# A six-layer cross network on one core: tiles of two groups woven at the start, output tails by one DMA turn and a Pool copy, fillers on TensorE, products moved in the last job

## The chip, the cores and the metric

The kernel runs on one core of a Trainium2 chip. The metric is device time in microseconds (us), less is better. A profile's span, from first to last instruction, is about 2 us shorter than the time of the same execution. The engines are called as in the profile: PE is TensorE (PEld its weight loads), ACT is ScalarE, DVE is VectorE, POOL is GpSimd, SP is SyncE, which here only issues DMAs.

## The reference, cut to what matters

```python
B, Din, L = 16384, 416, 6            # bf16 throughout
def reference(x0, ws, bs):           # x0 [B, Din], ws [L, Din, Din], bs [L, Din]
    x = x0
    for l in range(L):
        proj = jnp.einsum('bd,de->be', x, ws[l]) + bs[l]
        x = x0 * proj + x
    return x
```

## The kernel before: the parts that matter here

The batch is cut into 8 groups of 2048 rows. A *job* (g, l) is layer l of group g; the jobs are interleaved so that a group's next layer mostly finds its input done. The 416 features are three tiles of 128 and a *tail* of 32. A tile of a job, written (g, l)i, takes 12 full products of 128x512 on PE and 4 *row products* for the 32 tail inputs. Two neighbouring tiles share one stretch of row products. The tails of several jobs are computed together. ACT adds the bias while it empties PSUM; DVE multiplies by x0 and adds x.

```python
def load_group(g):                         # input, turned by DMA; SP issues in order
    for t in range(NT):
        add("sp", ... dma_start_transpose(x0s[s] tile t, x0[rows, t*P:(t+1)*P]))
    add("sp", ... dma_start_transpose(Tb[:, :], x0[rows, D - P:D]))
    for j in range(NJ):                    # four copies: the tail's quarters into place
        add("sp", ... dma_start(x0s[s][q, XW:XW + CH], Tb[P - T32:P, ...]))
...
load_nat(...)                              # group 0 comes in as rows and is turned on PE
load_w3(0, "sp"); load_wm(1, "sp"); load_w3(1, "sp"); load_group(1)
...
keep_busy(14, 7)                           # 14 products of no use, before the first input
def first_job(): ...                       # (0,0): turns, 3 tiles, then its tails
...
for jb in order[1:-1]:                     # order: (0,0), (0,1), (1,0), (0,2), (1,1), ...
    for i in range(NT): items.append(("tile", jb, i)) ...

def output(g):                             # groups 0 to 6: turn back by DMA, then store
    if g < LAST - 1: turn(0); turn(1)
    for j in range(NJ):                    # the tails: four turns of 32x512
        add("sp", ... dma_start_transpose(ost[:, j*KK:(j+1)*KK, NT*P:D], x3s[s3][q, :]))
    if g == LAST - 1: turn(0); turn(1)
    turn(2)
    add("sp", ... dma_start(out rows of g, ost))        # 1.66 MB
...
# the last job (7,5) is computed in row order, so that it can be stored without turns:
turn_main(0, bka, (0, 1)); turn_tails(0, bka)   # turns of x by PE
nat_rows(0, bkb, True)                          # row products and bias
turn_main(0, bka, (2,))                         # needs x tile 2, which is the last one made
rows_out(0, bka)                                # ACT and DVE copy the turned x out
layer_full(0, bkb)                              # 12 products, ACT copies, DVE multiplies and adds
turn_main(1, ...) ... layer_full(1) ... layer_full(2) ... layer_full(3), with stores between
```

A source line number differs between kernels when lines were added above it; the lines shown below name what they write and read.

## Time and profile before

| | before |
|---|---|
| time, median | 492.34 us at first (491.89 to 492.51), later runs 491.56 to 493.71 |
| PE busy, share of the span | 474.3 us, 97% |
| DVE, ACT, POOL busy | 405.8, 343.4, 11.9 us |
| steady state, two tiles | 5.29 us of full products and 0.54 us of row products |

The profile's page gives the span, the busy time of each engine and the shares of the chain of waits that ended last:

```profile
span 490.6 us, 8035 instructions
PE 474.3 (97%) x3191; PEld 203.2 (41%) x3245; DVE 405.8 (83%) x713; ACT 343.4 (70%) x372; POOL 11.9 (2%) x37
PE 90%; DVE 4%; ACT 2%; issue 2%; DMA 1%; SPq 0%; DVEq 0%
```

PE is the limit nearly everywhere, and a change that removes no products can only win where PE stands still or runs slowly. Those places are the two ends. The timeline has start, duration, engine, instruction and count, and in brackets the idle time before and what ended it. The start:

```profile
4.84 0.82 PE L516 MATMUL ps<-ident,x 128*128 128x128 bf16 x6 [0.60 <-DMA x<-in_x_dram]
8.53 1.49 PE L516 MATMUL ps<-ident,x 128*128 128x128 bf16 x12
10.28 0.84 PE L516 MATMUL ps<-ident,x 128*128 128x128 bf16 x12
...
20.79 0.83 PE L443 MATMUL ps<-x,wm 128*32 128x512 bf16 x12
25.77 0.61 PE L430 MATMUL ps<-x,w 32*128 32x512 bf16 x8 [0.41 <-DVE x L408]
26.32 5.35 PE L418 MATMUL ps<-x,wm 128*128 128x512 bf16 x23
43.04 0.40 PE L430 MATMUL ps<-x,w 32*128 32x512 bf16 x4 [0.35 <-DVE x L408]
```

The same twelve transposes take 1.49 us at 8.53 us and 0.84 us at 10.28 us: PE's clock rises between them. The first job's tail products start at 20.79 us. PE waits twice for an x-tail from DVE, before 25.77 us and before 43.04 us. The end:

```profile
463.50 5.00 SPq L604 DMA_TRANSPOSE ost<-x  x4
466.76 1.35 DVE L386 TENSOR_TENSOR tw<-tw,x 128x1024 bf16<-128x1024 bf16 x2
468.54 7.92 SPq L595 DMA_TRANSPOSE ost<-x  x3
470.73 0.86 ACT L753 ACTIVATE x<-ps 128x832 bf16<-128x832 bf16 x1 [1.02 <-PE ps L731]
472.93 2.10 ACT L789 ACTIVATE x<-ps 128x416 bf16<-128x416 f32 x4
476.02 1.62 ACT L753 ACTIVATE x<-ps 128x832 bf16<-128x832 bf16 x2 [0.99 <-PE ps L740]
478.72 0.37 SPq L617 DMA_DIRECT2D out_dram<-ost  x1
485.89 0.38 ACTq L803 DMA_DIRECT2D out_dram<-x  x1
```

SP issues seven output turns of group 6 in one row, from 463.50 to 476.46 us, and its store at 478.72 us, when the last job's own stores are about to begin. The last store is issued at 485.89 us, and the span still runs until 490.6 us. The DMA view of the last 15 us shows why (size, then us from issue to landing):

```profile
out_dram<-ost SPq DMA_DIRECT2D x1, 1664.0 KB, 6.7
out_dram<-x SPq DMA_DIRECT2D x1, 832.0 KB, 7.0
out_dram<-x SPq DMA_DIRECT2D x1, 104.0 KB, 4.5
out_dram<-x ACTq DMA_DIRECT2D x1, 104.0 KB, 3.8
```

A store of 104 KB needs 3.8 to 4.5 us. Group 6's own store has landed by then (478.72 + 6.7 = 485.4 us), but the last job's 832 KB had to queue with it and lands at 487.6 us, and the smaller stores come behind that. The DMA engines move about 350 GB/s from 480 to 489 us without a break.

### The profile page before, as it was taken

To read this page: it belongs to the slowest core of one execution; us is meant where nothing else is said; L and a number is where in the kernel's file an instruction comes from. 1 tells how busy PE (TensorE), PEld (TensorE's weight loads), DVE (VectorE), ACT (ScalarE), POOL (GpSimd) and SP (SyncE) were. 2 spreads that over 40 slices of the span, in tenths; PEclk is the share of its full clock that TensorE was granted. 3 is DMA by queue.
4 is the path that set the end of the run, shared out by engine and by line. 5 is a ranking of instruction groups with operands and counts; after the bars stand their busy time and mean duration, and the time that the engine had idled before them with its cause. 6 is when DMAs were issued, how large, how long until landed. Compare 5 with 4: busy or idle time off the path is not lost.

```text
span 490.6 us, 8035 instructions
## 1 busy us (share of the span) xinstructions
PE 474.3 (97%) x3191; PEld 203.2 (41%) x3245; DVE 405.8 (83%) x713; ACT 343.4 (70%) x372; POOL 11.9 (2%) x37
## 2 busy tenths in 40 slices
PE   7999999999999999999999999999999999999994
PEld 5333444444444444443444444434444443444352
DVE  1778888888888888888888888888888888888885
ACT  4576777677677677767677767767767676777773
POOL 1012200000000000000000000000000000000000
PEclk9999999999999999999999999999999999999998
DMA  8795982000001387359316952570000226035188
GB/s 251 141 181 139 176 129 66 1 1 0 2 0 36 63 225 141 50 117 243 54 22 115 232 95 51 118 252 1 1 1 1 43 57 179 17 74 153 43 137 278
DMA packets 126921, 47.65 MB, mean 97 GB/s; under 512 B 107674, under 2 KB 125476, under 8 KB 126884
## 3 DMA queue, kind: packets, MB, share of 16 engines
q1 hardware_dynamic: 126328, 46.71, 43.6%
q8 instruction: 25, 0.41, 0.4%
q10 hardware_dynamic: 556, 0.43, 0.3%
q14 instruction: 12, 0.10, 0.1%
HBM read 5.97 MB, written 13.63 MB: 40 GB/s over the span
## 4 chain that ended last, share of the span: by engine, by line
PE 90%; DVE 4%; ACT 2%; issue 2%; DMA 1%; SPq 0%; DVEq 0%
PE ps L418 72%; PE ps L430 8%; PE ps L443 5%; ACT tw L377 2%; DVE x L391 2%; PE ps L448 2%; DVE tw L386 1%; PE ps L761 1%; DMA x<-in_x_dram 1%; PE ps L516 1%; PE ps L731 0%; PE ps L521 0%; ACT ts L404 0%; ACT x L789 0%; DVE ts L406 0%
## 5 line engine op out<-in xcount | busy, mean ns | idle before, releaser
L377 ACT ACTIVATE tw<-ps,bias 128x1024 bf16<-128x1024 f32 (+1 forms) x295 | 299.5, 1070 | 129.2 <-PE ps L430 107.1
L418 PE MATMUL ps<-x,wm 128*128 128x512 bf16 x1638 | 373.6, 380 | 5.6 <-issue 3.3
L418 PEld LDWEIGHTS ps<-x,wm 128*128 128x128 bf16 x1692 | 159.0, 98 | 214.5 <-issue 28.4
L386 DVE TENSOR_TENSOR tw<-tw,x 128x1024 bf16<-128x1024 bf16 (+1 forms) x285 | 193.1, 682 | 65.2 <-ACT tw L377 65.0
L391 DVE TENSOR_TENSOR x<-tw,x 128x1024 bf16<-128x1024 bf16 (+1 forms) x285 | 181.4, 677 | 0.0
L430 PE MATMUL ps<-x,w 32*128 32x512 bf16 x564 | 44.5, 380 | 0.9 <-DVE x L408 0.8
L443 PE MATMUL ps<-x,wm 128*32 128x512 bf16 x564 | 38.7, 380 | 0.0
L404 ACT ACTIVATE ts<-ps,bias 128x512 bf16<-128x512 f32 x47 | 28.7, 700 | 0.0
L430 PEld LDWEIGHTS ps<-x,w 32*128 32x128 bf16 x564 | 9.1, 92 | 34.1 <-issue 32.6
L443 PEld LDWEIGHTS ps<-x,wm 128*32 128x32 bf16 x564 | 13.8, 96 | 15.7 <-issue 2.9
L408 DVE TENSOR_TENSOR x<-ts,x 128x512 bf16<-128x512 bf16 x47 | 18.5, 417 | 0.0
L406 DVE TENSOR_TENSOR ts<-ts,x 128x512 bf16<-128x512 bf16 x47 | 18.5, 417 | 0.0
L448 PE MATMUL ps<-x,wbd 128*32 128x512 bf16 x188 | 18.3, 379 | 0.0
L293 POOL COPY wbd<-w 32x32 bf16<-32x32 bf16 x24 | 9.8, 406 | 39.7 <-DMA w<-in_ws_dram 38.4
L529 DVE COPY x<-ps 128x512 bf16<-128x512 bf16 x4 | 1.7, 424 | 9.9 <-PE ps L521 9.9
L761 PE MATMUL ps<-wm,x 128*128 128x416 bf16 x48 | 9.2, 341 | 0.0
L526 ACT ACTIVATE x<-ps 128x512 bf16<-128x512 bf16 x8 | 4.3, 594 | 5.9 <-PE ps L516 5.9
L789 ACT ACTIVATE x<-ps 128x416 bf16<-128x416 f32 x15 | 7.4, 524 | 1.2 <-PE ps L761 1.1
L448 PEld LDWEIGHTS ps<-x,wbd 128*32 128x32 bf16 x188 | 5.0, 97 | 5.1
L791 DVE TENSOR_TENSOR x<-x,x 128x416 bf16<-128x416 bf16 x15 | 5.5, 371 | 1.9 <-ACT x L789 1.7
L761 PEld LDWEIGHTS ps<-wm,x 128*128 128x128 bf16 x48 | 5.1, 114 | 3.5 <-issue 1.0
L796 DVE TENSOR_TENSOR x<-x,x 128x416 bf16<-128x416 bf16 x16 | 5.6, 367 | 0.0
(36 smaller groups left out, 42.9 us busy)
## 6 DMA issues: line engine op xcount, KB each, us to landing
out_dram<-ost SPq DMA_DIRECT2D x7, 1664.0 KB, 6.8
x<-in_x_dram SPq DMA_DIRECT2D x7, 416.0 KB, 6.3
wm<-in_ws_dram SPq DMA_DIRECT2D x5, 312.0 KB, 3.1
x<-Tb SPq DMA_DIRECT2D x28, 32.0 KB, 1.8
out_dram<-x SPq DMA_DIRECT2D x1, 832.0 KB, 7.0
ost<-x SPq DMA_TRANSPOSE x49, 2.7
w<-in_ws_dram SPq DMA_DIRECT2D x24, 26.0 KB, 2.4
x<-in_x_dram SPq DMA_DIRECT2D x2, 208.0 KB, 3.1
```

What stands on the lines that cost most here:

```text
L293: add("pool", lambda h, q=q: h.tensor_copy(wbd[l][q, q], w3[l][q, NT * P:D]), reads=[("w3", l, j)], writes=[("wbd", l)])
L377: add("act", lambda h, a=a, w=w, b0=b0: h.activation(tw[r][:, a * CH:(a + w) * CH], psum[:, b0 * CH:(b0 + w) * CH], ACT_F.Identity, bias=b ...
L386: add("dve", lambda h, a=a, e=e: h.tensor_tensor(tw[r][:, a * CH:e * CH], tw[r][:, a * CH:e * CH], x0s[s0][:, i * GC + a * CH:i * GC + e * ...
L391: add("dve", lambda h, a=a, e=e: h.tensor_tensor(xs[so][:, i * GC + a * CH:i * GC + e * CH], tw[r][:, a * CH:e * CH], src(i, a, e), ALU.ad ...
L404: add("act", lambda h: h.activation(ts[r][:, :], bank(b), ACT_F.Identity, bias=bias[:, 3, l:l + 1], scale=1.0), reads=[("ps", b), "bias"], ...
L406: add("dve", lambda h: h.tensor_tensor(ts[r][:, :], ts[r][:, :], x0s[s0][:, XW:XW + CH], ALU.mult), reads=[("ts", r)] + x03_toks(s0), writ ...
L408: add("dve", lambda h: h.tensor_tensor(x3s[so][:, :], ts[r][:, :], src, ALU.add), reads=[("ts", r)] + stok, writes=[("x3", so)], hold=True)
L418: add("pe", lambda h, t=t, j=j: h.matmul(bank(banks[j]), wm[l][:, t, ecols], src(t, j, j + 1), start=(first and t == 0), stop=(not first a ...
L430: add("pe", lambda h, q=q, j=j: h.matmul(bank(banks[j]), w3[l][q, ecols], src[q, :], start=first, stop=not first, tile_position=(j * T32, 0)),
L443: add("pe", lambda h, t=t, j=j, src=src, l=l, b=b: h.matmul(bank(b, j * T32, (j + 1) * T32), wm[l][:, t, NT * P:D], src(t, j, j + 1), star ...
L448: add("pe", lambda h, j=j, s3=s3, l=l, b=b: h.matmul(bank(b, j * T32, (j + 1) * T32), wbd[l][:, j * T32:(j + 1) * T32], s3, start=False, s ...
L761: add("pe", lambda h, t=t: h.matmul(bank(b, n=D), xcol(t, j, kk), wm[l][:, t, :], start=(first and t == 0), stop=(not first and t == NT - 1)),
```

## The change

It has four parts, each meant to shorten one of the ends:

1. *Fillers:* eight 128x128 products of the identity between the two halves of the first input, where PE waits for DMA, to keep its clock from staying low.
2. *The weave:* the first tiles run as (1,0)0, (0,1)0, (1,0)1, tails, (0,1)1, (0,1)2, (1,0)2, so that (1,0)'s work stands where (0,1) waits for DVE. The tail's input Tb is turned second instead of last.
3. *The output turn:* a group's tails go through one turn of 128x512 into a new buffer and a Pool copy into place, instead of four turns of 32x512; tile 0 is turned first in every group.
4. *The last job:* the products of tiles 0 and 1 go ahead of the turns of x tile 2, for which PE waits.

```diff
@@ load_group @@
-        for t in range(NT):
-            add("sp", ... dma_start_transpose(x0s[s] tile t, ...))
+        turn(0)
         add("sp", lambda h: h.dma_start_transpose(Tb[:, :], x0[rows, D - P:D]), ...)
+        turn(1)
+        turn(2)
@@ transposed_chunk @@
-        for t, k in seq + [(NT, k) for k in range(KK)]:
+        for n, (t, k) in enumerate(seq + [(NT, k) for k in range(KK)]):
+            if j == 0 and n == NT * 2:
+                keep_busy(8, 3)
@@ output @@
-        if g < LAST - 1: turn(0); turn(1)          # (cut to one line)
-        for j in range(NJ):
-            add("sp", ... dma_start_transpose(ost[:, j * KK:(j + 1) * KK, NT * P:D], x3s[s3][q, :]))
-        if g == LAST - 1: turn(0); turn(1)
+        turn(0)
+        add("sp", lambda h: h.dma_start_transpose(ot3[:, :, :], x3s[s3][:, :]), ...)
+        add("pool", lambda h: h.tensor_copy(
+            ost[:, :, NT * P:D].rearrange("p (j k) f -> p j k f", j=NJ),
+            ot3[:, :, :].rearrange("p k (j f) -> p j k f", j=NJ)), ...)
+        turn(1)
         turn(2)
@@ items @@
-    for jb in order[1:-1]:
-        for i in range(NT): ...
+    where[((1, 0), 1)] = where.pop(((1, 0), 0))
+    tiles = [((1, 0), 0), ((0, 1), 0), ((1, 0), 1), ((0, 1), 1), ((0, 1), 2), ((1, 0), 2)]
+    tiles += [(jb, i) for jb in order[3:-1] for i in range(NT)]
@@ last job @@
     nat_rows(0, bkb, True)
+    for j in range(NJ):
+        nat_full(0, j, bkb[j], False, (0, 1))
     turn_main(0, bka, (2,))
     rows_out(0, bka)
-    layer_full(0, bkb)
+    layer_full(0, bkb, (2,))
```

## The prediction

> **What bounds the kernel now.** TensorE (PE). The page shows PE busy 474.3 of 490.6 us (97%), and the chain of waits is 90% PE. In the steady state a pair of tiles takes 5.29 us (24 full products) plus 0.54 us (8 row products), back to back. The change removes no steady-state product, so it can only win at the two ends, where PE is late. Four places:
>
> 1. *Clock at the start.* In the chain of waits three 128x512 products at 7.45 us take 1.28 us (427 ns each) and twelve transposes at 8.73 us take 1.28 us (107 ns each); at 10.35 us twelve take 0.78 us. PE runs at about half speed until about 10 us. The Trainium skill, "TensorE: Matmul & The Clock Gate", Part 1, says that the clock rises only after a window of about 3.4 us of sustained activity, on a free-running window. The timeline shows PE idle 0.60 us before 4.84 us (input DMA). Eight fillers there (107 ns each, 0.86 us by estimate) close that gap, cost about 0.26 us when cold, and should let the clock rise some 3 us earlier. That saves about 0.6 us on three products and 0.5 us on twelve transposes. Net estimate 0.7 us; it depends on the window's phase.
>
> 2. *The weave.* The timeline shows tile (0,1)0 starting at 21.77 us; its work (12 products, 8 row products) should take 3.1 us but the next full products start at 26.31 us: PE waits for the x-tail from VectorE (done 25.72 us). Later (0,2)0's row products wait for an x-tail (43.04 us, 0.35 us idle plus restart). With (1,0)0 first, its row products run in the gap, but (0,1)0's still wait for the same VectorE tail, so of the first gap only about 0.3-0.4 us returns; the second gap (0.5 us) vanishes, as three tiles then lie between. Sum 0.9 us. (1,0)0 now needs group 1's input by 21 us: Tb is turned second, the last input turn moves from third to fourth and should land near 21 us; there is over 1 us of slack before it matters.
>
> 3. *The last job.* PE waits for x at 470.4-472.1 us (four waits in the timeline). The eight t=0,1 products (1.5 us) move into it. ScalarE is then the limit (its evictions run 472.1-475.0 us without a gap), so the gain is its idle 0.99 us before the copy at 476.02 us: 0.95 us.
>
> 4. *The last stores.* Group 6's store is issued at 478.72 us since SP's seven output turns run back to back from 463.5 to 476.5 us (four of 1.24 us for tails). From 479.5 to 489.4 us the DMA engines move about 350 GB/s without a break: the end waits for bandwidth, too. With one tail turn instead of four, and tile 0 turned first, that store should go out about 4 us earlier, limited by x tile 2 ready at 469.3 us. The last stores then land in about 3 us instead of 3.8-4.5: gain 1.0 us. The Pool copy (128x512 strided, seven in all) is 1-2 us each by estimate, hidden behind turns 1 and 2.
>
> **Sum** about 3.5 us, nothing on steady-state PE: 488.7 us (range 487.2 to 490.3). Faster by over 2%: 0.01; within: 0.98; slower: 0.01.
>
> **Right or wrong is shown by:** start time of the product at 10.35 us and its pace; PE's waits for x-tails at 25 and 43 us; ScalarE's 0.99 us gap; issue time of group 6's store and GB/s in the last 10 us; steady-state pairs still 5.83 us.
>
> **What would make it wrong:** the fillers not warming the clock (0.3 us lost); group 1's input later than 22 us; (0,1)2 evicted too late for (0,2)0; Pool's copy slowing VectorE or delaying the store.

## The result, and the profile after

The changed kernel takes 488.26 us (median of four runs, 488.06 to 488.65), the kernel before 492.42 us in the runs beside it. Ratios here are from the fast runs of the same rounds, so not quite the ratio of the medians or of the means; this one is 0.9913, with an interval of 0.9893 to 0.9933. Executions over 1.5% slower than the fastest of the same kernel are left out of the means. The time lies in the predicted range, 0.4 us under the predicted 488.7 us. The page after:

```profile
span 486.5 us, 8047 instructions
PE 472.3 (97%) x3199; PEld 202.7 (42%) x3253; DVE 407.2 (84%) x713; ACT 343.1 (71%) x372; POOL 16.4 (3%) x44
PE 91%; SPq 3%; ACT 2%; issue 2%; DMA 1%; DVE 1%; DVEq 0%
```

The middle is as it was; the chain still gives two tiles 5.29 us of full products. The start, by the timeline:

```profile
4.85 0.55 PE L523 MATMUL ps<-ident,x 128*128 128x128 bf16 x6
7.62 0.84 PE L523 MATMUL ps<-ident,x 128*128 128x128 bf16 x12 [0.43 <-DMA x<-in_x_dram]
...
19.41 0.83 PE L448 MATMUL ps<-x,wm 128*32 128x512 bf16 x12
22.39 2.54 PE L423 MATMUL ps<-x,wm 128*128 128x512 bf16 x11 [1.93 <-DMA x<-in_x_dram]
24.86 0.61 PE L435 MATMUL ps<-x,w 32*128 32x512 bf16 x8
25.40 5.35 PE L423 MATMUL ps<-x,wm 128*128 128x512 bf16 x24
```

PE's clock goes to full speed at 4.94 us (the transposes start 107 ns apart before it and 56 ns apart after it), and the first job's tail products start 1.38 us earlier (20.79 to 19.41). Then there is a wait that the kernel before did not have: PE stands for 1.93 us until group 1's turned input lands, and (1,0)0 starts at about 22.2 us. (Its first product has no record, x11 instead of x12, so the true wait is nearer 1.7 us.) The waits for DVE's tails are gone. In the steady state after that PE is 1.45 us earlier than before: one stretch of 19 products, the same place in both chains, starts at 424.27 us before and at 422.82 us after.

The end:

```profile
462.08 1.99 SPq L607 DMA_TRANSPOSE ot<-x  x1
465.32 1.70 DVE L391 TENSOR_TENSOR tw<-tw,x 128x1024 bf16<-128x1024 bf16 x2
465.43 4.60 SPq L602 DMA_TRANSPOSE ost<-x  x2
465.64 0.84 POOL L609 COPY ost<-ot 128x512 bf16<-128x512 bf16 x1 [24.14 <-DMA ot<-x]
470.54 1.62 ACT L759 ACTIVATE x<-ps 128x832 bf16<-128x832 bf16 x2 [2.27 <-PE ps L737]
472.69 0.37 SPq L621 DMA_DIRECT2D out_dram<-ost  x1
473.63 1.68 ACT L759 ACTIVATE x<-ps 128x832 bf16<-128x832 bf16 x2
483.91 0.38 ACTq L809 DMA_DIRECT2D out_dram<-x  x1
```

Group 6's store goes out at 472.69 us instead of 478.72. The last store is issued 1.98 us earlier than before: 1.45 us from the start, 0.53 us from the last job. And the stores land quickly, by the DMA view of the last 16 us:

```profile
out_dram<-ost SPq DMA_DIRECT2D x1, 1664.0 KB, 6.7
out_dram<-x SPq DMA_DIRECT2D x1, 832.0 KB, 3.6
out_dram<-x SPq DMA_DIRECT2D x1, 104.0 KB, 2.0
out_dram<-x ACTq DMA_DIRECT2D x1, 104.0 KB, 2.0
```

From the last issue to the end of the span it is 2.54 us instead of 4.73: another 2.19 us. So the 4.17 us between the two spans are 1.45 at the start, 0.53 in the last job and 2.19 at the last stores.

### The profile page after: what moved, and what is told of

Its sections match the earlier page's. It is cut to its first block, busy times and chain, and to the rows that moved or that the text cites. A ratio compares the mean times of both kernels' runs of the same rounds, so it can differ in the third digit from the quotient of the medians.

```text
span 486.5 us, 8047 instructions
## 1 busy us (share of the span) xinstructions
PE 472.3 (97%) x3199; PEld 202.7 (42%) x3253; DVE 407.2 (84%) x713; ACT 343.1 (71%) x372; POOL 16.4 (3%) x44
## 4 chain that ended last, share of the span: by engine, by line
PE 91%; SPq 3%; ACT 2%; issue 2%; DMA 1%; DVE 1%; DVEq 0%
PE ps L423 73%; PE ps L435 8%; PE ps L448 6%; PE ps L453 2%; PE ps L767 1%; SPq L301 1%; DMA x<-in_x_dram 1%; SPq L287 1%; ACT tw L382 1%; SPq L306 1%; ACT x L795 1%; SPq L478 0%; ACT x L759 0%; PE ps L778 0%; DVE x L396 0%
## 5 line engine op out<-in xcount | busy, mean ns | idle before, releaser
L609 POOL COPY ost<-ot 128x512 bf16<-128x512 bf16 x7 | 4.8, 686 | 413.1 <-DMA ot<-x 413.1
L797 DVE TENSOR_TENSOR x<-x,x 128x416 bf16<-128x416 bf16 x15 | 5.5, 371 | 1.1 <-ACT x L795 1.0
```

## The experiments

All twelve runs are told here. Each was timed beside the kernel before. Where small differences are read, the mean of a kernel's own fast runs is given as well, because the kernel before scatters over 2 us and moves a ratio. The kernels come from four sets of rounds, on more than one chip; the mean of the kernel before lay between 492.60 and 492.68 us in each, so means of different sets are compared below with that much care.

### Each part alone

`fill_only` is the kernel before with this edit alone:

```diff
+            if j == 0 and n == NT * 2:
+                keep_busy(8, 3)
```

> The eight fillers alone. Theory (the fillers close the hole in TensorE's first busy stretch and the clock rises a window earlier): products at full pace by about 5 us, the first job's tail products start near 19.4 us instead of 20.8 us, and the whole 1.4 us passes to the end, since what follows waits on VectorE's chain of that job: about 491.0 us, 1.2 to 1.5 us under before. Rival (the early clock in the changed kernel was luck of a free-running window): start as before, 0 to 0.3 us slower.

`weave_only` has the new order of tiles and the new place of Tb's turn (the `load_group` and `items` parts of the diff).

> The weave of tiles and the new order of the group 1 input turns, without fillers. Theory: group 1's turned input lands near 22.1 us as in the changed kernel, 0.3 us later than TensorE could use it; (0,1)0 still waits for VectorE's x-tail of (0,0) at 25.7 us, so its full products begin near 26.2 us, 0.1 us earlier than before; the second wait (43 us) goes. Gain 0.5 to 0.6 us. Rival 1 (the weave is what gains at the start): 1.2 us or more. Rival 2 (it gains nothing): within 0.1 us.

`turn_only` has the `output` part of the diff.

> Output tails by one turn and the Pool copy alone. Theory (the end waits for DMA bandwidth because group 6's store is late): that store is issued about 4 us earlier (near 474.7 us), the last 104 KB stores land in about 2 us instead of 4, gain 1.7 to 2.1 us. Rival (the end is set by TensorE and VectorE, the stores are a fixed tail; the 2 us came from the last job's reordering): gain under 0.4 us.

`lastjob_only` has the `last job` part of the diff.

> The last job's products moved before the turns of x tile 2, alone. Theory: the last vector instruction is 0.5 us earlier, but the DMA engines are still busy with group 6's late store until the same time, so the end moves by 0 to 0.2 us. Rival (TensorE's chain decides the end): the full 0.5 us or more.

| part alone | mean of fast runs (range) | ratio to before, interval |
|---|---|---|
| fillers | 491.46 (490.21 to 491.96) | 0.9979, 0.9965 to 0.9992 |
| weave | 492.20 (491.55 to 493.02) | 0.9987, 0.9974 to 1.0001 |
| output turn | 490.74 (490.38 to 491.75) | 0.9958, 0.9944 to 0.9972 |
| last job | 493.00 (492.38 to 493.82) | 1.0004, 0.9990 to 1.0018 |

The output turn does what was expected of it: group 6's store is issued at 473.12 us, the 104 KB stores land in 2.1 us, and the gain of 0.0042 x 492.4 us = 2.1 us is the largest of the four. The last job's new order gains nothing alone, as expected, though by its profile PE comes 0.54 us earlier there once the later start of that execution (0.73 us) is taken off. Its stores show where that goes; DMA view of the last 22 us:

```profile
out_dram<-x SPq DMA_DIRECT2D x1, 832.0 KB, 8.4
out_dram<-x ACTq DMA_DIRECT2D x1, 104.0 KB, 5.1
```

They need longer than before, because group 6's store (issued at 480.20 us in this profile) is still ahead of them. The weave alone has its trace as expected only in part: the second wait for a tail is gone, and the full products after it start 0.9 us earlier (43.37 to 42.46), of which 0.15 us is an earlier start. But group 1's input, expected near 22.1 us, landed at 20.08 us, and PE did not wait for it. In time, 0.6 us is not clear of noise.

The fillers' profile showed more than was expected (tail products at 18.59 us, 2.2 us earlier), and their time less (1.0 us by the ratio). What clears this up is a look at all profiles together.

### When the clock rises

The trace records when PE's clock went to full speed. Here it is, with the start of the first job's tail products, in the profile of every kernel whose profiled execution was fast; us, on the timeline's scale (the times in the texts recorded before the runs, such as "near 5.1 us" and "472.6 to 476.0 us", are about 0.24 us too late on it):

| no fillers | rise | tail products | | with fillers | rise | tail products |
|---|---|---|---|---|---|---|
| before | 9.99 | 20.79 | | after | 4.94 | 19.41 |
| weave_only | 9.58 | 20.64 | | fill_only | 4.76 | 18.59 |
| turn_only | 8.12 | 19.92 | | fill_lastjob | 7.85 | 19.90 |
| lastjob_only | 11.41 | 21.52 | | fill_endfill | 7.38 | 19.61 |
| no_fill | 8.80 | 20.27 | | early_input | 5.54 | 18.90 |
| order_only | 10.94 | 21.23 | | early_two | 6.04 | 19.11 |
| mean | 9.81 | 20.73 | | mean | 6.09 | 19.25 |

The Trainium skill, "TensorE: Matmul & The Clock Gate", Part 1, says that the clock is decided on a window of 3413 ns that runs free of the kernel. The traces agree: the first stretch at full speed lasts 477.87 us (140 x 3.413) in nine of the twelve profiles, 481.28 us (141 x 3.413) in two and 464.21 us (136 x 3.413) in turn_only. In the table the rise falls anywhere in a stretch 3.3 us wide without fillers, in one 3.1 us wide with them, and on average 3.7 us earlier, about one window. Counting windows back from the rise shows why. The first two lines are of before, the third of after (us, then busy us and instructions of PE, PEld, DVE, ACT, POOL; the clock column reads 1.00 because the trace has no clock record before the first rise):

```profile
3.16:6.57 3.41, 2.81 (x28) 1.90 (x27) 0.33 (x1) 1.32 (x5) 0.00 (x0) 1.00 0.99 337
6.57:9.99 3.42, 3.42 (x24) 2.40 (x23) 0.41 (x2) 0.53 (x2) 0.00 (x0) 1.00 0.92 296
1.53:4.94 3.41, 3.15 (x29) 2.96 (x30) 0.00 (x0) 1.49 (x2) 0.40 (x2) 1.00 0.94 288
```

In all six profiles without fillers the window before the last one contains part of the hole that ends at 4.8 to 5.0 us, and the clock did not rise after it; with the hole closed, that window can already count. (Busy time alone is not the rule: 2.97 us of a window were enough in fill_only and 2.98 us were not in lastjob_only.) So the fillers do work, by one window, worth 1.5 us on the first job on average; but the two profiles that were compared first (9.99 and 4.94) differ by more than that by luck, and the profile of fill_only (4.76) is the luckiest of all: 5.05 us lie between that first pair, 3.7 us between the means.

The same clock can fall again. In the profile of turn_only it ran at half speed from 472.33 to 475.74 us, one window, after PE's waits in the last job. Busy time by stretch (us, then busy us and instructions of PE, PEld, DVE, ACT, POOL, then the granted clock, DMA share and GB/s):

```profile
468.92:472.33 3.41, 2.21 (x20) 1.12 (x18) 3.41 (x10) 1.67 (x2) 0.00 (x0) 1.00 1.00 188
472.33:475.74 3.41, 3.41 (x16) 1.79 (x14) 1.83 (x6) 1.94 (x5) 0.00 (x0) 0.50 0.59 187
```

That execution took 491.75 us; the other four took 490.38 to 490.61 us, with mean clocks of 0.998 and 0.999, which leave no room for a whole window at half speed in mid-run. So the fall cost about 1.3 us in one execution of five, as far as one execution can show.

### Which parts need each other

Four more kernels: fillers with the last job's order; fillers with 24 further fillers in the last job's hole, in place of its new order; output turn with the last job's order; and the whole change without fillers. The second one's edit, on top of fill_only:

```diff
     turn_tails(0, bka)
+    keep_busy(24, bkb[0])
     nat_rows(0, bkb, True)
```

> Fillers and the last job's new order together. In the run with fillers alone the profiled execution (490.21 us, mean clock 0.998) had no second half-speed stretch, while its four other executions (491.6 to 492.0 us) have a mean clock of 0.995; in the run with the output turn alone, the profile shows half speed from 472.6 to 476.0 us, after TensorE's waits in the last job. Theory (those waits let the clock fall in some executions; the last job's new order fills them): all five executions at 490.0 to 490.6 us with mean clock 0.997 or more. Rival (the parts simply add): 491.7 plus 0.0 to 0.2 us, spread as with fillers alone.

> As fillers alone, with 24 fillers put into the hole of the last job, ahead of its row products, while its order stays as before: nothing useful moves. Theory (it is the clock): no half-speed stretch at the end, all five executions at 490.0 to 490.7 us, as with the new order. Rival (it is the work moved into the hole): 491.7 us, as with fillers alone.

> Output turn and the last job's new order. Theory: with group 6's store out early the end follows TensorE's chain, so the last job's 0.5 us now counts, and the clock doesn't fall at the end: 489.6 to 490.1 us in all executions, against 490.4 to 491.75 us for the turn alone; the lastjob change, worth nothing alone, is worth 0.5 us or more here. Rival (last job's order is worth nothing anywhere): 490.5 us.

> The whole change without its eight fillers in the first chunk. Theory: the clock rises at 8 to 12 us instead of near 5.1 us, the first job ends 1.4 us or so later; but the whole change waits 1.9 us for group 1's input at 22.2 us, which the later start hides: 0.9 to 1.3 us slower than the whole change (489.1 to 489.5 us), with a wider spread. Rival (the fillers matter little, as alone): within 0.5 us of it.

| kernel | mean of fast runs (range) | ratio to before, interval |
|---|---|---|
| fillers + last job | 491.25 (490.79 to 491.67) | 0.9972, 0.9960 to 0.9984 |
| fillers + fillers at the end | 491.26 (490.77 to 491.94) | 0.9972, 0.9960 to 0.9984 |
| output turn + last job | 489.83 (489.34 to 490.63) | 0.9943, 0.9931 to 0.9956 |
| all without fillers | 488.88 (488.66 to 489.14) | 0.9924, 0.9912 to 0.9936 |

The first two missed what was expected: they came to 491.25 and 491.26 us instead of 490.0 to 490.6 and 490.0 to 490.7. My theory that fill_only's slower executions had lost the clock at the end falls as far as these runs go. Their low mean clock (0.995 to 0.996) also appears in fill_lastjob, whose profile has no second half-speed stretch before PE's work ends: there the clock falls at 485.71 us, when PE has finished. So the mean clock doesn't tell the two apart, and the fall of the clock is shown for one execution of turn_only only. What these runs do show is simpler: with group 6's store still late, neither the new order nor fillers at the end bring a difference that can be told from the noise.

The third confirms the coupling from the other side: behind the output turn the last job's new order is worth 490.74 - 489.83 = 0.9 us, or 0.7 us without the one execution in which turn_only's clock fell (490.49). Alone it was worth nothing.

The fourth is between theory and rival: the fillers are worth 488.88 - 488.31 = 0.6 us in the whole change. Its timeline at the start says why it isn't 1.5:

```profile
25.25 0.39 PE L435 MATMUL ps<-x,w 32*128 32x512 bf16 x4 [0.91 <-DVE x L413]
```

Without fillers PE begins (1,0)0 at 21.25 us without waiting for input and then waits 0.91 us for DVE. With them it waits 1.93 us for input and not for DVE. The limit has passed from DVE's tail to SP's input turns. How late these land differs between executions, though: with the same order of turns the last one lands at 20.08 us in weave_only, 21.20 us in no_fill and 22.11 us in after. Why is not known, so part of the 1.93 us may belong to that one execution.

### The output turn split, the weave taken out, and the input brought forward

`order_only` keeps the four tail turns and only changes the order:

```diff
-        if g < LAST - 1:
-            turn(0)
-            turn(1)
+        turn(0)
         for j in range(NJ): ...            # the four tail turns
-        if g == LAST - 1:
-            turn(0)
-            turn(1)
+        turn(1)
         turn(2)
```

> The kernel before, its four tail turns kept, only the order of the output turns changed (tile 0, tails, tile 1, tile 2 for every group). Splits the output part: is it the fewer turns, or the turn of tile 0 that no longer waits behind the tails in the last of these groups? Theory (both: three tail turns of 1.24 us less, and tile 0 turned while SP was idle): group 6's store goes out near 475 us, 1.5 to 2 us later than with one turn, and the time gains 1.0 to 1.6 us of the 1.9. Rival (fewer turns is all of it): gain under 0.5 us.

It takes 492.03 us (491.59 to 492.44), ratio 0.9982 (0.9967 to 0.9997), a gain of 0.9 us by the ratio and 0.7 by the medians, less than my theory wanted. The store did not move as expected; timeline:

```profile
464.44 5.62 SPq L602 DMA_TRANSPOSE ost<-x  x4
470.10 4.60 SPq L595 DMA_TRANSPOSE ost<-x  x2
478.72 0.37 SPq L613 DMA_DIRECT2D out_dram<-ost  x1
```

SP has issued the last turn by 474.70 us, but it lands only 4.0 us later, where before it was 2.3 us (476.46 to 478.72). In that time the DMA engines moved 13 GB/s from 474.50 to 476.00 us and 57 GB/s from 477.20 to 478.70 us, against about 210 GB/s while they turn; the kernel before has one such stall (12 GB/s from 475.50 to 476.75 us). Each stall begins when the core's instruction queue moves 8 or 16 KB, and all seven fast profiles with four tail turns have one while turns of tiles are under way. With one tail turn the turns have landed, or nearly, when that transfer comes. Whether it causes the stall was not tested. PE is 0.42 us later in this execution than in the profile of before, so the store gained 0.4 us, not 2. So the order alone does not make the store early; one turn instead of four together with the Pool copy does (473.12 us in turn_only). How much of that is issue time and how much the stall stays open.

`no_weave` is the whole change without its `load_group` and `items` parts.

> The whole change without the weave and the new order of input turns. Theory: the start is then bound by VectorE's chain of the first job alone, so the fillers count fully (1.4 us under the 489.8 us of output turn and last job without fillers), both waits for x-tails (1.4 us before 25 us, 0.35 us before 42 us) are back: 488.4 to 488.9 us, so the weave is worth 0.2 to 0.6 us in the whole change. Rival (the weave adds its 0.9 us in full): 489.1 us or more.

It takes 488.54 us (488.25 to 488.86, four fast runs), ratio 0.9913 (0.9897 to 0.9929). Against 488.31 us for the whole change, the weave is worth 0.2 us, within the noise; without fillers it was worth 489.83 - 488.88 = 0.95 us. And the fillers without the weave are worth 489.83 - 488.54 = 1.3 us, with it 0.6. Each has nearly its predicted or a greater value where the other is missing, and together they bring 489.83 - 488.31 = 1.5 us.

`early_input` is the whole change with group 1's turns ahead of layer 1's weights; `early_two` adds another order of tiles:

```diff
-    load_wm(1, "sp")
-    load_w3(1, "sp")
-    load_group(1)
+    load_group(1, lambda: (load_wm(1, "sp"), load_w3(1, "sp")))   # called after turn(2)
@@ early_two also @@
-    tiles = [((1, 0), 0), ((0, 1), 0), ((1, 0), 1), ...
+    tiles = [((1, 0), 0), ((1, 0), 1), ((0, 1), 0), ...
```

> The whole change, with group 1's four input turns issued ahead of layer 1's weights on SP. Theory (TensorE's 1.9 us wait at 22.2 us is for input that SP issues too late): that wait is gone, (1,0)0 starts at 20.0 to 20.5 us; then (0,1)0's row products wait for VectorE's x-tail near 24.3 us: 0.3 to 0.7 us under the whole change, 487.6 to 488.0 us. Rival (the input isn't what holds it, VectorE is): no gain.

> As early_input, with (1,0)0 and (1,0)1 both ahead of (0,1)0. Theory: nothing on TensorE waits for VectorE's tail any more; the row products of the first pair start as soon as (1,0)0's full products are done, near 23 us instead of 24.9 us: 1.2 to 1.9 us under the whole change, 486.4 to 487.1 us. Rival (another limit stands close behind: group 1's x-tail copies, landing near 23 us, or ScalarE's and VectorE's backlog): as early_input.

| kernel | mean of fast runs (range) | ratio to before, interval |
|---|---|---|
| whole change | 488.31 (488.06 to 488.65) | 0.9913, 0.9893 to 0.9933 |
| early_input | 487.61 (487.42 to 487.79) | 0.9894, 0.9878 to 0.9910 |
| early_two | 487.11 (486.83 to 487.25) | 0.9884, 0.9868 to 0.9899 |

The wait for input was real: with it gone PE starts (1,0)0 at 20.1 us and the kernel gains 0.7 us. It doesn't wait for DVE then, as I had expected, but 0.84 us for the copies of Tb, which SP issues last. In early_two, which asks nothing of DVE's tail, the same copies are the next limit; timeline:

```profile
20.32 2.54 PE L425 MATMUL ps<-x,wm 128*128 128x512 bf16 x11 [0.16 <-ACT tw L384]
23.07 0.61 PE L437 MATMUL ps<-x,w 32*128 32x512 bf16 x8 [0.22 <-DMA x<-Tb]
```

It is the fastest kernel, correct like the others, 1.2 us under the change and 5.6 us under the kernel before by the medians (487.17 against 492.77). Its median lies 0.07 us above the range that was expected.

## Why the prediction was right, point by point

The sum was right: 3.5 us predicted by the four terms, 4.16 us measured between the medians. The terms were not all right, and they did not simply add.

- *The clock, 0.7 us.* Mechanism right, size too small and not constant. Fillers bring the rise one window earlier, 3.7 us on average. The cost of 0.26 us for slow fillers is not to be seen: where the clock rose late (fill_endfill, fill_lastjob) the next transposes start at 4.90 and 5.00 us, and without fillers they start anywhere from 4.80 to 5.02 us. The fillers are worth 1.5 us on the first job and 1.3 us in time beside the two end parts, but 0.6 us in the whole change.
- *The weave, 0.9 us.* Right where the start is late (0.95 us without fillers), wrong in the whole change (0.2 us). The step that failed is "the last input turn moves from third to fourth and should land near 21 us; there is over 1 us of slack before it matters". It landed at 22.11 us (20.08 and 21.20 us in two other executions with this order), and the fillers had used the slack: PE was ready 1.4 us sooner and stood for 1.93 us. The prediction named "group 1's input later than 22 us" as a way to fail, but added the two gains as if they were independent. Clock and weave together were to bring 1.6 us and brought 1.45 us in the traces, 1.5 us in the times.
- *The last job, 0.95 us.* It measured 0.53 us in the trace. The step that failed is "ScalarE is then the limit ..., so the gain is its idle 0.99 us". In the kernel before ACT makes its first copy at 470.73 us, inside PE's hole. With the products moved ahead of the turns of tile 2, that copy too comes behind them (470.54 us, which is 1.26 us late against a start that is 1.45 us earlier). The idle time before the second copies is gone, as predicted, but ACT then works without a break and PE waits 0.3 us for a bank that ACT still empties (at 473.85 us).
- *Pool's copy.* It took 0.69 us (mean of seven). The prediction had it hidden; it isn't quite. While the last of them runs, DVE's pair of multiplications takes 1.70 us, in all five fast profiles with this copy (after, turn_only, no_fill, early_input, early_two), and 1.35 or 1.36 us in all seven without it. The Trainium skill, "GPSIMD Engine Reference", Specifications, says that POOL's SBUF interfaces are shared with DVE, with contention where a DVE instruction has two SBUF inputs; this agrees. In turn_only these multiplications lie on the chain that ends last, so the 0.35 us counts there; in the whole change that chain runs through PE instead (464.56 to 470.51 us), so there it does not. No run kept the one turn and moved the copy alone, so it is the two together that are shown to do this.
- *The last stores, 1.0 us.* Mechanism right, size half: the output turn alone gained 2.1 us, and from last issue to end of span it went from 4.73 to 2.54 us. The term assumed that the last stores would land in about 3 us; with group 6's 1.66 MB out of the way they landed in 2.0 us. The Trainium skill, "DMA: Bandwidth & Descriptors", Anatomy of one DMA, gives about 2.0 us of fixed cost for one DMA (measured there on another queue kind); 2.0 us for 104 KB is close to that, so little can have been left to wait for.
- *The steady state* stayed as predicted: 5.29 us for 24 full products, before and after.

So the errors partly cancelled: the stores brought 1.2 us more than predicted, the last job 0.4 us less and the start 0.15 us less.

## What to carry to other kernels

Gains at one end of a kernel that each remove a different wait don't add: the earliest part to get ready stands at whichever wait is longest, so ask after each what stands next (here first VectorE's tail, then the input turns, then the tail's copies). The reordering at the very end was worth nothing while a big store was still in the DMA queues, and 0.7 to 0.9 us once that store had gone early, so free the queues first. With one profile per kernel, check the time at which the clock rose before reading a start-up difference of a microsecond or two.

## What the Trainium skill lacked or had wrong

- "TensorE: Matmul & The Clock Gate": it states that the clock falls after an idle window of about 3.4 us, and advises against idle gaps of over 3 us between bursts of products; its passage on a second failure mode adds that frequent short idle times can do it too, without a share. In turn_only the clock fell to half speed for 3.41 us at the end of a window in which the profile has PE busy 2.21 of 3.41 us and no single gap over 0.5 us. A partly idle window was enough there, but not always: in lastjob_only PE was busy 1.77 of 3.42 us from 482.45 to 485.87 us, and the clock held for another window. What decides it no run here settles.
- The same page says that the point of the rise varies by 500 ns either way with the window's phase; here it varied over 3.3 us without fillers and 3.1 us with them. The page doesn't say what closing one gap is worth. Here closing 0.6 us of idle time, with 8 products, brought the rise 3.7 us earlier on average (six profiles against six).
- "DMA: Bandwidth & Descriptors" has no measured cost of issuing DMA turns of SBUF to SBUF of these sizes on this chip. Here four turns of 32x512 took 5.0 to 5.6 us on SP back to back and one of 128x512 took 1.2 to 2.0 us. The last turn landed 2.3 us after SP had issued it before, 2.7 us in after and 4.0 us in order_only.
- No page gives a cause for executions that are slow from start to end with one core in use: one of turn_lastjob took 621.05 us with a mean granted clock of 0.756, and one of no_weave 1733.32 us with PE busy 98% of the span and products of 128x512 mostly 840 ns apart (216 ns in before), while their other executions took 489.3 to 490.6 and 488.3 to 488.9 us.
